# Linear attention and a gated MLP in one kernel: one more unit loaded by squares, six weight sums placed later, and two more decayed keys turned through DRAM

## The chip, the cores and the metric

The kernel runs on one core of a Trainium2 chip. The engines are TensorE (PE in the profile), VectorE (DVE), ScalarE (ACT), GpSimd (POOL) and SyncE (SP); SP, ACT and POOL also issue DMA transfers. The metric is device time in microseconds. Three executions of the kernel before gave 600.44, 600.48 and 600.49 us, median 600.48. A further execution was taken with the hardware profiler.

## The reference

The inputs q, k, v and f_logit have the shape (4 batches, 8 heads, 768 positions, 48 columns). With f = sigmoid(f_logit), every head keeps a 48 by 48 state and gives

```python
for t in range(S):
    state = f[:, :, t, :, None] * state + np.einsum('bhd,bhe->bhde', k[:, :, t], v[:, :, t])
    y[:, :, t] = np.einsum('bhd,bhde->bhe', q[:, :, t], state)
```

The outputs of the 8 heads are laid side by side, which gives x with 3072 tokens and 384 columns, and then

```python
g = x @ w_gate                      # 384 -> 1536
silu = g * (1.0 / (1.0 + np.exp(-g)))
val = x @ w_val                     # 384 -> 1536
return (silu * val @ w_out)         # 1536 -> 384
```

The three weight matrices come as 64-bit floats. The kernel converts them to 32-bit floats on the chip.

## The kernel before, in words

**Units.** The 768 positions are cut into 6 chunks of 128. A unit is one chunk of one batch, so there are 24 units; unit u has chunk u // 4 and batch u % 4 (B = 4). The second chunk holds units 4 to 7, the third units 8 to 11. The 8 heads of a unit are handled as 4 pairs (HP = 4).

**Attention of a unit.** `attention(u)` (L560) is a generator; its parts between two `yield`s are placed one by one. The gates f and their products along the chunk are needed with the head's columns on the partitions and time along the free dimension. The work in order: sigmoid of f (L601 or L608, ScalarE); a scan from the right, "tails" (L630, VectorE) and a reciprocal (L633); kT = k times tails (L576); a scan from the left, "gates" (L658); qT = q times gates (L576); the scores sc = kT by qT (L676, TensorE); the mask A = sc times causal (L691, VectorE, two instructions); y from the carried state (L712) and from A and v (L716, or L737 for the last batch of a chunk); the state's increment dS = kt by v (L757), where kt is the decayed k turned back to time on the partitions; and the new state (L764, L766). "least" (L656 or L683) is a small copy of the chunk's whole decay, from which `decay` makes "decayed". The outputs y reach the layout of the MLP's input xT through DRAM (L720 copies and L727 DMAs, 'xT<-yT'), while the last batch of a chunk goes through a "diagonal" tile (L737).

**Two ways to load.** A plain unit loads f, k and q with time on the partitions (L455) and TensorE transposes them: fTp, kTp and qTp (L596, four instructions each, one for a head pair). A unit "by squares" loads each of f, k and q with four DMAs into squares of 32 rows (L447), and VectorE transposes the squares (L611 for f, L622 for k, L662 for q). `by_squares(u)` is `u >= SQUARES * B - 2`, with SQUARES = 2, so units 6 and up. Loads by squares of units 6 and 7 are issued by POOL, those of later chunks by SP. All v loads but those of units 6 and 7 are issued by SP. A queue's transfers are issued in program order.

**Two ways to turn the decayed k.** Unless `turned` holds, TensorE transposes kT into a bank ("kt", L680, four instructions) and ScalarE copies it out (L689). Where it holds (units 6 and 7, and the fourth and fifth chunk), VectorE transposes kT by squares (L646), four DMAs write it to DRAM ("turn", L649) and one DMA loads it back as kt (L687). `turn_queue` is POOL for the second chunk and SP later.

**The weights.** A piece of the 64-bit weights is loaded by SP into one of four buffers (w64). ScalarE makes two tiles of it, "up" (L489) and "top" (L491), from two buffers each; VectorE joins them by a clamp (L500), a shift (L502), a 16-bit mask (L504) and an add (L506). In the profile these carry the output names w_both (w_gate and w_val together) and w_out. `weights()` issues one piece's fetch, one piece's sizes (ScalarE) and one piece's join (VectorE).

**The MLP.** For the first chunk, `mlp_plain` runs products x by w_gate and x by w_val (L812: 12 of each, three matmuls of 128 by 512 per product, into four banks), silu (L822), the multiplication h = silu times val (L826), and then down products (L835). From the second chunk on, `mlp_fifteen` makes the products of three blocks by three blocks with 15 instead of 18 products (L1014), from sums of the input (xs) and sums of the weights; `down_seven` (L1113, L1176) does the down product with 7 instead of 8. The sums of the weights are VectorE's: `weight_sums(odd)` lists 16 for each half (into "extra" and in place into w_both), and `down_weight_sums` lists four for w_out (ws1, ws2, w_out, ws4).

**What sets the order.** Up to the first three products of the first MLP, an order written out by hand is kept on all engines (`in_order(mark, ...)`). Then `take_turns` runs the steps of `mlp_plain(0)`, with `weights` between them, in turn with the steps of the second chunk's attention; the scheduler may move instructions there, and `keep_order` adds dependencies that hold some of them in order. `behind` holds the instructions of a step behind the VectorE instruction traced last. Three pairs of weight sums are inserted among the h products, the other 13 pairs are woven into the last steps of the down product. From the third chunk on, the order comes from due times: SCORES gives each unit's time and bank kind for its scores ("b", "o" or "A"), CHAINS the times of the steps before, DOWN_SUMS_AT those of the four w_out sums, and `times(c)` the rest; `down[i]` is the i-th half step of the down product. All four lists of steps are merged by time.

Of the kernel before, what the change touches and what calls it, by code (L numbers as in the profile page):

```python
# [9 lines left out]
FP32 = mybir.dt.float32  # L10
# [280 lines left out]
def short_path(ctx, tc, ident, least, judge, q, k, v, f_logit, moe_w_gate, moe_w_val, moe_w_out, out):  # L291
# [9 lines left out]
    nc = tc.nc  # L301
    B, H, S, D = q.shape
    C = 128
    NCH = S // C
    HP = H // 2
# [58 lines left out]
    def pairs(t, off=0):  # L364
        return t[:, off:off + HP * N1].rearrange("p (a t) -> p a t", t=N1)
# [33 lines left out]
    rooms = {nm: t.rearrange("p n h w -> p (n h w)")[:, 0:Q + HP * RUN] for nm, t in both_raw.items()}  # L399

    def by_squares(u):
        return u >= SQUARES * B - 2

    def make_rooms(pool):
        for nm in "fkq":
# [21 lines left out]

    traced = nc.cur_bb.bb.instructions
    by_pool = []

    def load(u, what="fkqv"):
        b, c = units[u]
        rows = slice(c * C, (c + 1) * C)
        inputs = dict(f=f_logit, k=k, q=q, v=v)
        for nm in "fqkv" if c >= SQUARES else "fvkq" if by_squares(u) else "fkqv":
            src = inputs[nm]
            if nm not in what:
                continue
            if nm == "v":
                dst = v_of(u)  # L440
            elif not by_squares(u):
                dst = raw[nm][u % NRAW]
            else:
                since = len(traced)
                for n in range(4):
                    at = Q * (1 - n % 2)
                    (nc.sync if c >= SQUARES else nc.gpsimd).dma_start(  # L447
                        out=rooms[nm][Q * n:Q * (n + 1), at:at + HP * RUN].rearrange("t (a e) -> t a e", a=HP),
                        in_=src[b, n // 2::2, rows, :].rearrange("a (t i) d -> t a (i d)", i=NI))
                if c < SQUARES:  # L450
                    by_pool.extend(ins for ins in traced[since:] if ins.engine == mybir.EngineType.Pool)
                    keep_order(by_pool[-5:])
                continue
            queue = nc.gpsimd if c < SQUARES and by_squares(u) else nc.sync
            queue.dma_start(out=dst[:, :, 0:D], in_=src[b, :, rows, :].rearrange("h t d -> t h d"))  # L455

    def weight_piece(dst, src, parts):

        b, a, n = dst.shape[1:]
        if src.dtype == FP32:
            by_row = src.rearrange("p a (b n) -> p a b n", n=n)
            return (lambda: [nc.sync.dma_start(out=dst[:, :, i], in_=by_row[:, i]) for i in range(a)]), [], []
        shape = [128, b // parts, a, n]
        kept = {}

        def fetch():  # L470
            kept["w"] = wst.tile([128, a, 2 * b * n], I32, tag="w64", name="w64", bufs=4)
            nc.sync.dma_start(out=kept["w"], in_=src)

        def part(m):
            return slice(m * b // parts, (m + 1) * b // parts)

        def halves(m):
            words = kept["w"].rearrange("p a (b n two) -> p a b n two", two=2, n=n)[:, :, part(m)].rearrange("p a b n two -> p b a n two")
            return words[:, :, :, :, 0], words[:, :, :, :, 1]

        def high_ends(m):
            quarters = kept["w"].bitcast(U16).rearrange("p a (b n four) -> p a b n four", four=4, n=n)[:, :, part(m)]
            return quarters.rearrange("p a b n four -> p b a n four")[:, :, :, :, 3]

        def sizes(m):
            lo, hi = halves(m)
            up = wst.tile(shape, I32, tag="up", name="up", bufs=NPART)
            ends = up.bitcast(U16).rearrange("p b a (n two) -> p b a n two", two=2)
            nc.scalar.activation(ends[:, :, :, :, 0], lo.bitcast(U32), AF.Copy, scale=2.0 ** -29)  # L489
            top = wst.tile(shape, I32, tag="top", name="top", bufs=NPART)  # L490
            nc.scalar.activation(top.bitcast(FP32), hi.bitcast(FP32), AF.Abs)  # L491
            kept["up", m], kept["top", m] = up, top

        def join(m, what=("clamp", "add")):
            lo, hi = halves(m)
            up, top = kept["up", m], kept["top", m]
            if "add" in what and "clamp" not in what:
                nc.vector.tensor_tensor(dst[:, part(m)].bitcast(I32), top, up, ALU.add)
                return
            nc.vector.tensor_scalar(top.bitcast(FP32), top.bitcast(FP32), as_float(0x38000000), as_float(0x47F00000),  # L500
                                    op0=ALU.max, op1=ALU.min)
            nc.vector.tensor_scalar(top, top, 3, 0x3FFFFFFF, op0=ALU.logical_shift_left, op1=ALU.bitwise_and)  # L502
            ends = up.bitcast(U16).rearrange("p b a (n two) -> p b a n two", two=2)
            nc.vector.tensor_single_scalar(ends[:, :, :, :, 1], high_ends(m), 0xC000, op=ALU.bitwise_and)  # L504
            if "add" in what:
                nc.vector.tensor_tensor(dst[:, part(m)].bitcast(I32), top, up, ALU.add)  # L506

        return fetch, [lambda m=m: sizes(m) for m in range(parts)], [lambda *what, m=m: join(m, *what) for m in range(parts)]
# [51 lines left out]
    def attention(u):  # L560
# [51 lines left out]
            load_after(u, "f")  # L612
        yield

        turned = SQUARES < c < NCH - 1 or c < SQUARES and in_squares
        turn_queue = nc.sync if c >= SQUARES else nc.gpsimd
        kT = att.tile([128, HP, C], FP32, tag="kT", name="kT")
        qT = att.tile([128, HP, C], FP32, tag="qT", name="qT", bufs=2)
# [9 lines left out]
        for part in parts:  # L628
            at = slice(part.start * N1, part.stop * N1)
            nc.vector.tensor_tensor_scan(tail[:, at][:, ::-1], gate[:, at][:, ::-1], floor[:, at][:, ::-1], 1.0,  # L630
                                         op0=ALU.mult, op1=ALU.max)
        whole = pairs(tail)[:, :, 1:2]
        nc.vector.reciprocal(pairs(start)[:, :, 0:1], whole)  # L633
        yield
# [18 lines left out]

        if in_squares:

            nc.scalar.copy(least[:, u, :], whole.rearrange("p a t -> p (a t)"))  # L656
            whole = least[:, u, :].unsqueeze(2)
        nc.vector.tensor_tensor_scan(gate[:, 0:n], gate[:, 0:n], start, 1.0, op0=ALU.mult, op1=ALU.add)  # L658
        yield
        if in_squares:  # L660
            qp = tail[:, 0:HP * C]
# [1 line left out]
            load_after(u, "qv" if c < SQUARES else "q")  # L663
        yield
        multiply(qT, qp, pairs(gate)[:, :, 1:N1])
        nc.gpsimd.memset(pairs(gate)[:, :, 0:1], 0.0)  # L666
        if c < SQUARES:
            decay()
# [8 lines left out]
        if c < NCH - 1 and not turned:  # L677
            p = bank("kt")
            for a in range(HP):
                nc.tensor.transpose(p[:, a * C:(a + 1) * C], kT[:, a, :], ident)  # L680
        yield
        if not in_squares:
            nc.scalar.copy(least[:, u, :], whole.rearrange("p a t -> p (a t)"))  # L683
        if c < NCH - 1:
            kt = att.tile([128, HP * C], FP32, tag="kt", name="kt")
            if turned:
                turn_queue.dma_start(out=kt, in_=turn.rearrange("t i a r e -> i t (a r e)"))  # L687
            else:
                nc.scalar.copy(kt, p)  # L689
# [73 lines left out]
        if c == 0:  # L763
            nc.scalar.copy(states[b], dS)  # L764
        elif c < NCH - 1:
            nc.vector.tensor_tensor(states[b], decayed[:, :, 0:D], dS, ALU.add)  # L766
        yield

    def load_after(u, what):
# [36 lines left out]
    def mlp_plain(c):  # L806
# [17 lines left out]
        def val(j):  # L824
            p = product(w_val, j, "val")
            nc.vector.tensor_tensor(part(j), part(j), p, ALU.mult)  # L826

        return ([lambda j=j, f=f: f(j) for f, j in ((gate, 0), (val, 0), (gate, 1), (val, 1))] +
                [lambda j=j, f=f: f(j) for i in range(2, NF, 2) for f in (gate, val) for j in (i, i + 1)],
# [49 lines left out]
    def chain(k, q, qmul, turn=None, head=None):  # L879
# [3 lines left out]
    between = [n * TRIPLE - 0.05 for n in range(NJ)]  # L883
    down = [NJ * TRIPLE + n * DOWN / 2 - 0.05 for n in range(14)]
    SCORES = {c: scores for c, scores in zip(range(2, NCH), (
        ((12, "b"), (between[2], "o"), (down[2], "A"), (down[6], "A")),
        ((PRODUCT - 0.05, "b"), (between[1], "o"), (between[3], "o"), (down[3], "A")),
        *[((down[10] - whole, "A"), (between[1], "o"), (between[3], "o"), (down[3], "A"))] * (NCH - 4)))}
    CHAINS = {c: chains for c, chains in zip(range(2, NCH), (
# [18 lines left out]
        return {"o": banks_o, "A": banks_a}[kind].tile([128, 512], FP32, tag=kind, name="sc")  # L908

    FINISH = (3, 5, 6, 7, 9, 10)  # L910
    DOWN_SUMS_AT = (13.1, 26.5, 38, 48)
    sums = {}

    def plus(dst, a, b):
# [278 lines left out]
    def behind(f):  # L1193

        n = len(traced)
        last = next(ins for ins in reversed(traced) if ins.engine == mybir.EngineType.DVE)
        f()
        keep_order([last] + [ins for ins in traced[n:] if ins.engine == mybir.EngineType.DVE])

    def take_turns(first, second, rest):  # L1200

# [77 lines left out]
    joins.pop(0)()  # L1279
    hidden[1]()  # L1280
    weights()
    load(B + 1)
    hidden[2]()
    steps.pop(0)()
    in_order(mark, (mybir.EngineType.PE, mybir.EngineType.DVE, mybir.EngineType.Activation, mybir.EngineType.SP))
# [5 lines left out]
    for i in range(len(joins) - hidden.count(weights)):  # L1291
        last.insert(3 * i, weights)
    sums_of = [weight_sums(odd) for odd in range(2)]
    for n, at in enumerate((5, 6, 8)):
        hidden.insert(hidden.index(weights, 3 * at), lambda n=n: behind(lambda: [t[n]() for t in sums_of]))
    take_turns(hidden + weave(last, sums_of[0][3:7] + sums_of[1][3:7] + sums_of[0][7:] + sums_of[1][7:]), steps, 8)
    assert not fetches and not joins

    early.close()
# [126 lines left out]
```

## Time and profile before

| what | value |
|---|---|
| median of three executions | 600.48 us |
| the profiled execution | 600.68 us |
| its span | 599.0 us |
| TensorE busy | 588.3 us (98%) |
| VectorE busy | 481.7 us (80%) |
| ScalarE busy | 293.6 us (49%) |
| GpSimd busy | 94.3 us (16%) |
| mean granted TensorE clock | 0.999 of full speed |

The span is the time from the first to the last record of the profiled execution; 1.7 us of that execution's time lie around it. Busy time of TensorE is modelled and pipelined, so that a matmul's start to the next one's start tells its price better than its duration. A number in square brackets at the end of a line of the timeline is the idle time of the engine before that instruction, with what released it.

By its own timeline, the first chunk's attention fills TensorE up to 29.07 us, the first MLP's gate and val products run from there to 101.93 us, its down products from 101.93 to 140.22 us, and the 15-product stages follow. The second chunk's attention lies among the first MLP's products: unit 5's f transposes at 55.35, its k and q transposes at 70.93, its scores at 77.47 and its kt transposes at 78.56 us; unit 6's scores at 104.60, unit 7's at 121.06. In the third chunk, unit 10's scores are at 204.38 and unit 11's at 215.94 us.

### The profile page before, as it was taken

What the parts mean: (1) busy time and instruction counts of PE and PEld (TensorE: products, weight loads), DVE (VectorE), ACT (ScalarE), POOL (GpSimd) and SP (SyncE); (2) the same over time, 40 slices, a digit from 0 to 9 for tenths busy, and PEclk for the clock granted to TensorE, in tenths of its full rate; (3) what the DMA queues carried; (4) which work ended last, traced back from release to release, by engine and by line L of the source; (5) the groups of instructions that cost most, each with busy time, mean ns of one, the idle gap of its engine ahead of it and who ended that gap; (6) DMA issues with size and microseconds to landing.
All of it is one profiled execution on the core that took longest, in us unless ns stands there. A gap on an engine that the chain in (4) does not pass through costs nothing.

```text
span 599.0 us, 10862 instructions
## 1 busy us (share of the span) xinstructions
PE 588.3 (98%) x3996; PEld 485.4 (81%) x3996; DVE 481.7 (80%) x834; ACT 293.6 (49%) x558; POOL 94.3 (16%) x211
## 2 busy tenths in 40 slices
PE   7899999999999999999999999999999999999996
PEld 5744545667888899888899888899988899988896
DVE  7999998978999977998995978995878972666731
ACT  3577854115776422576740566632376730356600
POOL 1102225100030230121130030320030320000000
PEclk9999999999999999999999999999999999999999
DMA  9999664124331244442344432343230100100001
GB/s 198 252 274 319 199 182 116 25 77 132 81 83 49 51 110 112 133 97 70 98 116 108 126 76 68 98 112 99 82 102 26 28 10 6 54 1 1 1 1 55
DMA packets 104058, 57.33 MB, mean 96 GB/s; under 512 B 65632, under 2 KB 95712, under 8 KB 104000
## 3 DMA queue, kind: packets, MB, share of 16 engines
q1 hardware_dynamic: 95552, 46.09, 29.3%
q0 software_dynamic: 6432, 7.75, 4.4%
q10 hardware_dynamic: 2016, 2.75, 1.3%
q8 instruction: 32, 0.52, 0.4%
q14 instruction: 26, 0.21, 0.1%
HBM read 46.27 MB, written 7.34 MB: 90 GB/s over the span
## 4 chain that ended last, share of the span: by engine, by line
PE 86%; DVE 0%; issue 0%
PE o L1113 20%; PE A L1014 18%; PE B L1014 14%; PE c L1014 6%; PE o L1014 6%; PE o L835 5%; PE sc L676 3%; PE o L1176 3%; PE y L716 2%; PE gate L812 2%; PE val L812 2%; PE y L737 1%; PE y L712 1%; PE dS L757 1%; PE kt L680 0%; DVE A L691 0%
## 5 line engine op out<-in xcount | busy, mean ns | idle before, releaser
L727 POOL DMA_DIRECT2D xT<-yT x120 | 60.0, 507 | 51.0 <-ACT yT L720 45.2
L1014 PE MATMUL A<-xs,w_both 128*128 128x256 f32 x240 | 62.2, 382 | 0.0
L1113 PE MATMUL o<-w_out,h 128*128 128x192 f32 x360 | 62.0, 327 | 0.0
L1113 PEld LDWEIGHTS o<-w_out,h 128*128 128x128 f32 x360 | 58.7, 190 | 1.2 <-DVE h L966 0.3
L1019 ACT COPY c<-A 128x512 f32<-128x512 f32 x40 | 23.3, 583 | 60.7 <-PE A L1014 60.7
L1019 ACT COPY aside<-A 128x512 f32<-128x512 f32 x60 | 35.2, 586 | 34.1 <-PE A L1014 33.9
L915 DVE TENSOR_TENSOR c<-c,aside 128x512 f32<-128x512 f32 x60 | 41.1, 685 | 12.2 <-ACT aside L1019 10.7
L1014 PEld LDWEIGHTS A<-xs,w_both 128*128 128x128 f32 x240 | 44.9, 190 | 6.6
L966 DVE TENSOR_TENSOR h<-h,c 128x256 f32<-128x256 f32 x100 | 40.5, 414 | 7.6 <-ACT h L1030 7.3
L691 DVE TENSOR_TENSOR A<-sc,causal 128x512 f32<-128x512 f32 x48 | 31.0, 686 | 15.7 <-PE sc L676 15.7
L918 DVE TENSOR_TENSOR c<-c,aside 128x512 f32<-128x512 f32 x60 | 41.0, 683 | 2.2 <-ACT aside L1019 2.1
L1030 ACT ACTIVATE h<-c 128x256 f32<-128x256 f32 x100 | 39.2, 416 | 6.6 <-DVE c L915 5.1
L1113 PE MATMUL o<-ws,h 128*128 128x192 f32 x240 | 41.5, 328 | 0.2 <-DVE A L691 0.2
L666 POOL MEMSET gates<- 128x4 f32 x24 | 3.1, 128 | 243.7 <-DVE qT L576 237.5
L1014 PE MATMUL B<-xs,w_both 128*128 128x256 f32 x160 | 41.2, 380 | 0.0
L1014 PE MATMUL A<-xs,extra 128*128 128x256 f32 x160 | 41.2, 380 | 0.0
L1014 PE MATMUL c<-xT,w_both 128*128 128x256 f32 x160 | 41.1, 379 | 0.0
L1014 PE MATMUL B<-xT,extra 128*128 128x256 f32 x160 | 41.1, 379 | 0.0
L1113 PEld LDWEIGHTS o<-ws,h 128*128 128x128 f32 x240 | 39.1, 190 | 0.8 <-DVE A L691 0.4
L1019 ACT COPY aside<-B 128x512 f32<-128x512 f32 x60 | 35.1, 585 | 8.3 <-PE B L1014 7.1
L918 DVE TENSOR_TENSOR c<-o,c 128x512 f32<-128x512 f32 x40 | 27.4, 685 | 12.6 <-ACT h L1030 6.6
L915 DVE TENSOR_TENSOR c<-c,o 128x384 f32<-128x384 f32 x15 | 8.3, 552 | 36.3 <-PE o L1113 36.3
(154 smaller groups left out, 1224.3 us busy)
## 6 DMA issues: line engine op xcount, KB each, us to landing
fsquares<-in_f_logit_dram SPq DMA_DIRECT2D x64, 96.0 KB, 2.4
qsquares<-in_q_dram SPq DMA_DIRECT2D x64, 96.0 KB, 2.2
ksquares<-in_k_dram SPq DMA_DIRECT2D x64, 96.0 KB, 2.4
w<-in_moe_w_gate_dram SPq DMA_DIRECT2D x6, 768.0 KB, 6.2
w<-in_moe_w_val_dram SPq DMA_DIRECT2D x6, 768.0 KB, 5.3
w<-in_moe_w_out_dram SPq DMA_DIRECT2D x6, 768.0 KB, 6.9
v<-in_v_dram SPq DMA_DIRECT2D x22, 192.0 KB, 3.0
out_dram<-ob ACTq DMA_DIRECT2D x14, 192.0 KB, 2.0
```

What stands on the lines that cost most here:

```text
L676: nc.tensor.matmul(sc[par][:, a * C:(a + 1) * C], lhsT=kT[r, a, :], rhs=qT[r, a, :], start=True, stop=True)
L691: nc.vector.tensor_tensor(A[:, par], sc[par].rearrange("p (a t) -> p a t", t=C), causal.unsqueeze(1).broadcast_to((128, HP, C)), ALU.mult)
L727: (nc.gpsimd if c >= SQUARES else nc.sync).dma_start(out=xT[c][f % 128:f % 128 + n, f // 128, b * C:(b + 1) * C], in_=yT[r:r + n, par, a / ...
L812: nc.tensor.matmul(p, lhsT=w[:, j, i, :], rhs=xT[c][:, i, :], start=(i == 0), stop=(i == KT - 1))
L835: nc.tensor.matmul(p, lhsT=hidden_tile(h, n // 2)[:, n % 2 * 2 + b // 2, b % 2 * C:(b % 2 + 1) * C], rhs=w_out[:, j, :], start=(n == 0), s ...
L915: nc.vector.tensor_tensor(dst, a, b, ALU.add)
L918: nc.vector.tensor_tensor(dst, a, b, ALU.subtract)
L966: lagging.append(lambda: f(*args))
L1014: nc.tensor.matmul(p[name][:, n, :], lhsT=weights_of[a][:, n, j, :], rhs=tokens[b], start=fresh and n == 0, stop=True, skip_group_check=True)
L1019: nc.scalar.copy(t, p[name])
L1030: nc.scalar.activation(dst, src[:, 0, :], AF.Silu)
L1113: nc.tensor.matmul(p[:, n, :], lhsT=lhsTs[j][:, n * C:(n + 1) * C], rhs=rhs[:, j, :], start=first and j == order[0] and n == 0, stop=j == ...
```

## The change

- `by_squares` holds from unit 5 on, so unit 5 (the second chunk's second batch) is loaded by squares. Its three sets of transposes on TensorE and its kt transposes fall away; POOL issues its 12 square loads, and its kT is turned through DRAM on POOL's queue as for units 6 and 7. The "least" copy of units by squares in the second chunk goes from ScalarE to VectorE.
- v of units 1 to 9 is loaded by POOL's queue.
- The first three pairs of weight sums leave the h products and are woven with the others behind the last h. Dependencies put unit 7's right-hand scan behind the last but one h, its left-hand scan behind the last h, and the woven sums from unit 6's new state on behind unit 7's qT. The 16-bit masks of w_out's joins stand behind unit 5's qT.
- `turned` holds for units 10 and 11 too, on SP's queue. For turned units of the third chunk and later, but for the last batch, the kt load is issued with the scores instead of a step later.
- Unit 11's scores have the due time of `down[5]` instead of `down[6]`; the w_out sums have the due times 1.4, 13.1, 26.5 and 48 instead of 13.1, 26.5, 38 and 48.

```diff
     def by_squares(u):
-        return u >= SQUARES * B - 2
+        return u >= SQUARES * B - 3
...
-            queue = nc.gpsimd if c < SQUARES and by_squares(u) else nc.sync
+            queue = nc.gpsimd if nm == "v" and 0 < u < SQUARES * B + 2 else nc.sync
             queue.dma_start(out=dst[:, :, 0:D], in_=src[b, :, rows, :].rearrange("h t d -> t h d"))
...
             nc.vector.tensor_single_scalar(ends[:, :, :, :, 1], high_ends(m), 0xC000, op=ALU.bitwise_and)
+            for ins in first_scores if n == DM else ():
+                keep_order([ins, traced[-1]])
...
-        turned = SQUARES < c < NCH - 1 or c < SQUARES and in_squares
+        turned = SQUARES * B + 2 <= u < (NCH - 1) * B or c < SQUARES and in_squares
...
                                          op0=ALU.mult, op1=ALU.max)
+        if u == SQUARES * B - 1:
+            keep_order([last_of_h[0], traced[-1]])
...
-            nc.scalar.copy(least[:, u, :], whole.rearrange("p a t -> p (a t)"))
+            (nc.scalar.copy if c >= SQUARES else nc.vector.tensor_copy)(least[:, u, :], whole.rearrange("p a t -> p (a t)"))
...
         nc.vector.tensor_tensor_scan(gate[:, 0:n], gate[:, 0:n], start, 1.0, op0=ALU.mult, op1=ALU.add)
+        if u == SQUARES * B - 1:
+            keep_order([last_of_h[1], traced[-1]])
...
         multiply(qT, qp, pairs(gate)[:, :, 1:N1])
+        if u == SQUARES * B - 1:
+            for ins in woven_sums[since[0]:]:
+                keep_order([traced[-1], ins])
+        if u == B + 1:
+            first_scores.append(traced[-1])
...
+        if c < NCH - 1:
+            kt = att.tile([128, HP * C], FP32, tag="kt", name="kt")
+        at_once = turned and c >= SQUARES and b < B - 1
+        if at_once:
+            turn_queue.dma_start(out=kt, in_=turn.rearrange("t i a r e -> i t (a r e)"))
         yield
...
-        if c < NCH - 1:
-            kt = att.tile([128, HP * C], FP32, tag="kt", name="kt")
+        if c < NCH - 1 and not at_once:
...
             nc.vector.tensor_tensor(states[b], decayed[:, :, 0:D], dS, ALU.add)
+            if u == SQUARES * B - 2:
+                since.append(len(woven_sums))
...
             nc.vector.tensor_tensor(part(j), part(j), p, ALU.mult)
+            if j >= NF - 2:
+                last_of_h.append(traced[-1])
...
-        ((12, "b"), (between[2], "o"), (down[2], "A"), (down[6], "A")),
+        ((12, "b"), (between[2], "o"), (down[2], "A"), (down[5], "A")),
...
-    DOWN_SUMS_AT = (13.1, 26.5, 38, 48)
+    DOWN_SUMS_AT = (1.4, 13.1, 26.5, 48)
...
-        keep_order([last] + [ins for ins in traced[n:] if ins.engine == mybir.EngineType.DVE])
+        sums = [ins for ins in traced[n:] if ins.engine == mybir.EngineType.DVE]
+        keep_order([last] + sums)
+        keep_order([last_of_h[-1], sums[0]])
+        woven_sums.append(sums[0])
...
-    load(B + 1)
     hidden[2]()
...
-    for n, at in enumerate((5, 6, 8)):
-        hidden.insert(hidden.index(weights, 3 * at), lambda n=n: behind(lambda: [t[n]() for t in sums_of]))
-    take_turns(hidden + weave(last, sums_of[0][3:7] + sums_of[1][3:7] + sums_of[0][7:] + sums_of[1][7:]), steps, 8)
+    take_turns(hidden + weave(last, sums_of[0][0:7] + sums_of[1][0:7] + sums_of[0][7:] + sums_of[1][7:]), steps, 8)
```

In the resulting instruction order TensorE makes unit 5's scores one gate product later than before and its y and dS two products later; unit 6's scores come after two down steps instead of one, and unit 7's after seven instead of six.

More of the change, by code (lines that the diff above doesn't have):

```diff
@@ L429, in short_path @@
     by_pool = []
+    first_scores = []
+    last_of_h = []
+    woven_sums = []
+    since = []
     def load(u, what="fkqv"):
```

## The prediction

> **What bounds the kernel now.** I read the page's busy shares and its closing chain first, then TensorE's waits, then the timelines at the places the diff touches. The page:
>
> ```profile
> PE 588.3 (98%) x3996; PEld 485.4 (81%) x3996; DVE 481.7 (80%) x834; ACT 293.6 (49%) x558; POOL 94.3 (16%) x211
> ...
> PE 86%; DVE 0%; issue 0%
> ```
>
> TensorE is the bound, and the chain is its instruction stream. The waits of TensorE (us in total, times, longest) show how little it loses:
>
> ```profile
> PE idle L362 <- DVE floor L354: 2.1, 1, 2.1
> PE sc L676 <- DVE qT L576: 1.9, 2, 1.1
> PE sc L676 <- ACT least L683: 0.5, 1, 0.5
> PE sc L676 <- ACT state L764: 0.4, 1, 0.4
> PE sc L676 <- ACT top L491: 0.3, 1, 0.3
> PE y L737 <- issue: 0.3, 1, 0.3
> PE o L1113 <- DVE A L691: 0.2, 1, 0.2
> ```
>
> All but two of these lie before 29.07 us. So time falls only where TensorE instructions or the two later waits go, and rises where a new wait appears. TensorE's timeline (start, duration, instruction):
>
> ```profile
> 55.35 0.60 PE L596 MATMUL fTp<-idf,fraw 128*128 128x128 f32 x4
> ...
> 70.93 0.60 PE L596 MATMUL kTp<-idf,kraw 128*128 128x128 f32 x4
> 71.37 0.60 PE L596 MATMUL qTp<-idf,qraw 128*128 128x128 f32 x4
> ...
> 77.47 1.16 PE L676 MATMUL sc<-qT,kT 48*128 48x128 f32 x16 [0.35 <-ACT top L491]
> 78.56 0.66 PE L680 MATMUL kt<-idf,kT 128*128 128x128 f32 x4
> ...
> 205.47 0.66 PE L680 MATMUL kt<-idf,kT 128*128 128x128 f32 x4
> ...
> 217.03 0.66 PE L680 MATMUL kt<-idf,kT 128*128 128x128 f32 x4
> 217.87 0.92 PE L1113 MATMUL o<-ws,h 128*128 128x192 f32 x4 [0.19 <-DVE A L691]
> ```
>
> These transposes are what the change removes. Matmuls overlap, so the price is start to next start.
>
> **TensorE, removed.** For unit 5 the f transposes cost 55.78−55.35 = 0.43, k and q 71.81−70.93 = 0.88, kt 79.05−78.56 = 0.49. For unit 10 kt costs 205.97−205.47 = 0.50. For unit 11 kt and the wait behind it run from 217.03 to 217.87, 0.84. That wait goes too: sc of unit 11 now comes a down step (2.03) earlier, and half a step on the o bank stands between it and the step that needs the masked A bank. The 0.35 before sc of unit 5 goes, because sc stands one product (2.58) later. Sum 3.49, say 3.5 us.
>
> **VectorE around unit 5.** Added: the f transpose 0.95, and k, q and the turn at 0.62 each, together 2.8; three "least" copies (0.10 to 0.2 each on ACT's rows) 0.3 to 0.6. Moved away: six sums of 0.60, 3.6. Net, it is no fuller before the last h; cost 0. The new pair of order there keeps the u16 parts (0.49) of w_out's joins behind qT of unit 5. In the new order they stand later anyway, and sc of unit 5 has 2.58 more, so 0; 0.4 if qT is still late (the row of the wait that goes).
>
> **The six sums behind the last h.** They add 3.6 us to VectorE where it idled (start, duration, [idle before, releaser]):
>
> ```profile
> 105.79 1.29 DVE L691 TENSOR_TENSOR A<-sc,causal 128x512 f32<-128x512 f32 x2 [2.91 <-PE sc L676]
> ...
> 129.91 0.35 DVE L766 TENSOR_TENSOR state<-decayed,dS 128x192 f32<-128x192 f32 x1 [3.62 <-PE dS L757]
> ```
>
> Idle 2.91+3.62 = 6.53, so 2.9 is left. Without that cover the masks of units 6 and 7 and the xs sums before 140.22 come late, one for one. The tail scan and gate scan of unit 7 now wait for h products; behind them stand its q transpose and qT, read by sc at 121.06, over 10 us after. Cost 0. The down sum moved to 1.4 falls into idle of 0.37 and 0.73 before the ob copies (139.13, 140.42): 0.
>
> **Units 10 and 11.** VectorE does one more transpose (0.62) for each; each unit's four turn DMAs and kt load join SP's queue. SP carries no v loads up to unit 9 any more, and the kt load is issued with the scores. A turn lands 2.3 after issue, a kt load in 5.8 at most: 8.1. From sc to dS of unit 10 is 204.38 to 215.38 less 0.50, 10.5 us; for unit 11 it is 13 or more. Cost 0. But qT of unit 11 ended at 213.06, now 0.62 later, 213.68, and sc arrives at 215.94−0.50−2.03 = 213.41. VectorE gets about 0.6 back from a sum moved out of this stretch. Ends 0 and 0.35 (0.27 and a latency); I take 0.1, near the balance.
>
> **ACT: the step I distrust.** ACT gives up unit 5's gates and kt copy and takes a table load, a sigmoid and another switch early, about 1.28+0.63+1.28 = 3.2, into idle of 1.67+1.51 at 41.85 and 43.56: 0. Later, in the new order, the last but one w_out piece's up and top, a table load, unit 7's sigmoid and a table load all stand ahead of the silu that frees a bank (of four) for a gate product. Rows of ACT's timeline before:
>
> ```profile
> 86.50 1.08 ACT L489 ACTIVATE up<-w 128x768 uint16<-128x768 uint32 x1 [4.61 <-DVE w_both L506]
> ...
> 90.47 0.60 ACT L822 ACTIVATE h<-gate 128x512 f32<-128x512 f32 x1
> 91.08 1.28 ACT L601 ACT_TABLE_LOAD   x1
> 92.38 0.63 ACT L601 ACTIVATE fraw<-fraw 128x512 f32<-128x512 f32 x1
> ```
>
> Start to start: up 0.92, top 0.83, load 1.30, sigmoid 0.53, load 1.30, silu 0.48, 5.36 together. The gate product before was the one at 91.52+2.58 = 94.10. It now stands before y and dS of unit 5 (2.07), and 0.43+0.88+0.49+0.35 = 2.15 is gone ahead of it: 89.88. So up must start by 84.5. It needs the piece landed. SP issues that piece behind the last xT DMA of unit 4, which shares a semaphore with a weight load issued near 70; that lands 6.9 later, the rest of the queue follows, and I place the piece's issue at 78.8 (77.8 to 80). The DMA rows of 54 to 105 us (KB each, median us to landing):
>
> ```profile
> w<-in_moe_w_out_dram SPq DMA_DIRECT2D x6, 768.0 KB, 6.9
> fraw<-in_f_logit_dram POOLq DMA_DIRECT2D x8, 96.0 KB, 5.5
> ```
>
> 78.8+6.9 = 85.7, so TensorE waits 1.2 at that gate. Ends: 0 (landing by 84.5) and 2.8 (issue 80, landing 0.4 above the median). I take 1.2.
>
> **POOL and the start.** POOL's queue takes 12 square loads, one turn and kt load, and v of units 1 to 5, 8 and 9. Unit 5's f is issued near 32; at 5.5 it lands near 38, before ACT's gap. v1 to v3 now run beside f1 to q2. Before, the first 20 us moved 230 GB/s on one queue, so three v (192 KB, 0.85 each) take 2.6 us of the engines; f2 landed at 10.29 and is read at 12.37. With all 2.6 ahead of it, 12.85: 0.5 late. But SP's queue sheds v1, and a wait of 0.48 at 15.08 absorbs a slip. I take 0; ends −0.1 and +0.5.
>
> [...]
>
> **Sum.** −3.5+1.2+0.1 = −2.2. The profiled execution took 600.68 (span 599.0 and 1.7 around), 0.2 above the median of 600.48; it becomes 598.5, the median 598.3.
>
> **Rivals.**
> No new wait (the piece lands by 84.5): −3.5+0.1, 597.1. For it: ACT was idle 4.61 before 86.50, so it isn't short of time. Against: that piece must land 5.2 us before ACT's old reading of it.
> Gain given back: the wait is 2.8 and unit 11's 0.35 and the start's 0.5 come with it: −3.5+3.65 = +0.15, 600.6, within what this measurement can tell from no change (0.2%, 1.2 us).
> Slower: POOL's square loads. The sigmoids of units 6 and 7 stand in ACT's queue ahead of silus that free TensorE's banks. If POOL's loads land 5.5 later than 5.5 after issue, that is past ACT's idle (4.61), and each microsecond more is TensorE's. At 5 us later the gain is spent (−3.5 against the weights' 2.8 and 0.7 here); at 6 to 7, about +1.3 to +2.5, 602 to 603. For it: 16 more transfers on a queue that already takes 5.5. Against: unit 5's have long landed when unit 6's are issued.
>
> **How the numbers follow.** Forecast (0.4 to 2.4 of wait) 0.50; no new wait 0.24; gain given back 0.13; slower 0.13. The forecast's own range is 597.4 to 599.4. The range reaches from 596.7 (no wait, the start 0.1 better, 0.3 for unlisted idle) to 600.7, leaving out the slower case and a little of the low end. Faster by over 0.2% (below 599.28) takes the no-wait case and nearly all of the forecast, 0.73; same 0.14; slower 0.13.
>
> **What would show it.** In the changed kernel's profile: no kt, kTp or qTp group on TensorE for unit 5; no wait of sc on ACT top and none of o on A; near 89 us a gate product waiting for an ACT silu by about 1.2, and ACT's up before it released by a weight DMA. The VectorE idle before state of unit 7 should fall below 1.5 with no TensorE wait between 100 and 140. The first gate product should still start within 0.5 of 29.07. I am wrong if TensorE waits for sc of unit 7, for the first 15-product stage at 140, or for A or kt of units 10 and 11, or if 29.07 slips more.

## The result, and the profile after

The changed kernel took 607.75 us (606.87 to 607.94, four runs) against 600.49 us for the kernel before in the same comparison: a ratio of 1.0116, with a 95% interval of 1.0104 to 1.0128. The prediction was 598.3 us with a range up to 600.7; the kernel became 7.3 us slower instead of 2.2 us faster.

(A correction to the description ahead of the prediction: the transfers 'xT<-yT' go from on-chip memory to on-chip memory; DRAM takes no part in them. Nothing in the prediction's numbers rests on it.)

The page of the changed kernel (busy time per engine, then the rows of TensorE and of its granted clock in 40 slices of 15.2 us):

```profile
PE 590.9 (97%) x3972; PEld 484.5 (80%) x3972; DVE 485.6 (80%) x843; ACT 291.5 (48%) x552; POOL 111.2 (18%) x235
...
PE   7899987999999999999999999999999999999996
...
PEclk9999996999999999999999999999999999999999
```

TensorE executes 24 instructions less and is 2.6 us longer busy. TensorE's row dips in the sixth and seventh slice, 76 to 106 us, and the clock's in the seventh. TensorE's waits (us in total, times, longest) name it:

```profile
PE gate L833 <- DVE h L847: 3.5, 1, 3.5
PE gate L833 <- ACT h L843: 2.3, 1, 2.3
PE idle L362 <- DVE floor L354: 2.1, 1, 2.1
PE sc L691 <- DVE qT L582: 1.1, 2, 0.8
PE fTp L602 <- DMA fraw<-in_f_logit_dram: 0.8, 2, 0.5
```

The two upper lines are new. So is the last one, which lies in the first 20 us and belongs to the start. The two waits that were to go, 0.3 before unit 5's scores and 0.2 before o at 217.87, are gone as forecast. TensorE's timeline there (start, duration, instruction, [idle before, releaser]):

```profile
82.36 5.31 PE L833 MATMUL val<-xT,w_both 128*128 128x512 f32 x12
89.95 4.54 PE L833 MATMUL gate<-xT,w_both 128*128 128x512 f32 x6 [2.27 <-ACT h L843]
97.94 5.49 PE L833 MATMUL gate<-xT,w_both 128*128 128x512 f32 x6 [3.45 <-DVE h L847]
103.36 0.79 PE L731 MATMUL y<-qT,decayed 48*64 48x128 f32 x16
```

The two gate products behind the waits last 4.54 and 5.49 us; two such products together took 5.42 before, at 91.52. The windows of TensorE (stretch, busy time, granted clock, DMA share, GB/s) tell why:

```profile
89.00:90.00 1.00, 0.05 (x1) 1.00 0.21 80
90.00:91.00 1.00, 1.00 (x2) 0.51 0.05 18
...
94.00:95.00 1.00, 0.49 (x2) 1.00 0.00 0
...
96.00:97.00 1.00, 0.00 (x0) 0.92 0.32 66
97.00:98.00 1.00, 0.06 (x1) 0.50 0.34 74
102.00:103.00 1.00, 1.00 (x2) 0.50 0.77 184
104.00:105.00 1.00, 1.00 (x24) 1.00 0.08 25
```

The clock is granted at 0.50 with the end of the first wait and from inside the second on, and stays there for 3.4 and 6.8 us. So a wait is paid twice here: once as idle time, once in the matmuls behind it.

Held against the trace of before at the same instructions, the account is this. The first gate product is 0.28 late. Unit 5's removed work and wait give 0.43+0.88+0.49+0.35 = 2.15. The waits take 2.27+3.45 = 5.72. The slow matmuls take 4.54−2.74 = 1.80, then (103.36−97.94)−2.58 = 2.84, then 0.12 in y: 4.76. That makes +8.6; the first 15-product stage starts at 149.09 instead of 140.22, +8.88 (the 0.3 left over I put down to the ends of matmuls, from which the two waits are counted: the two gate products at 79.05 of before last 5.32 by their ends and 5.16 from start to start). Units 10 and 11 give 1.36 back by 237 us, which leaves +7.52, and the rest of the span gives back 0.4: the spans differ by 606.1−599.0 = 7.1.

What held the two gate products? ScalarE's and VectorE's timelines of the changed kernel:

```profile
79.81 0.93 ACT L495 ACTIVATE top<-w 128x768 f32<-128x768 f32 x1
87.62 1.06 ACT L493 ACTIVATE up<-w 128x768 uint16<-128x768 uint32 x1 [6.89 <-DMA w<-in_moe_w_out_dram]
88.55 0.86 ACT L495 ACTIVATE top<-w 128x768 f32<-128x768 f32 x1
89.31 0.59 ACT L843 ACTIVATE h<-gate 128x512 f32<-128x512 f32 x1
```

```profile
84.73 0.14 DVE L664 COPY least<-tails 128x4 f32<-128x4 f32 x1
89.44 0.56 DVE L504 TENSOR_SCALAR top<-top 128x768 f32<-128x768 f32 x1 [4.58 <-ACT top L495]
...
97.21 0.67 DVE L847 TENSOR_TENSOR h<-h,val 128x512 f32<-128x512 f32 x1
```

ScalarE's in-order queue waits 6.89 us for the fourth w_out piece, and the silu behind it (89.31), whose gate product had ended at 78.67, is what the first late gate product needs. VectorE waits in turn 4.58 us for that piece's top; behind it stand unit 6's chain and more joins, and only then the ninth h product (97.21), which frees the bank of the last gate product; its silu had ended at 89.90 and its val product by 87.67. SyncE's queue shows when the piece was issued (start, time until the last of the group is issued):

```profile
56.00 14.64 SPq L476 DMA_DIRECT2D w<-in_moe_w_out_dram  x3
70.84 6.88 SPq L746 DMA_DIRECT2D xT<-yT  x10
77.82 1.89 SPq L476 DMA_DIRECT2D w<-in_moe_w_out_dram  x3
```

Three w_out pieces go out ahead of unit 4's ten xT transfers and three behind them; in the kernel before it was four and two:

```profile
55.56 11.66 SPq L472 DMA_DIRECT2D w<-in_moe_w_out_dram  x4
68.46 8.15 SPq L727 DMA_DIRECT2D xT<-yT  x10
76.73 1.04 SPq L472 DMA_DIRECT2D w<-in_moe_w_out_dram  x2
```

### The profile page after: what moved, and what is told of

It is laid out like the page before. It is cut to its first block, busy times and chain, and to the rows that moved or that the text cites. A ratio compares the mean times of both kernels' runs of the same rounds, so it can differ in the third digit from the quotient of the medians.

```text
span 606.1 us, 10863 instructions
## 1 busy us (share of the span) xinstructions
PE 590.9 (97%) x3972; PEld 484.5 (80%) x3972; DVE 485.6 (80%) x843; ACT 291.5 (48%) x552; POOL 111.2 (18%) x235
## 4 chain that ended last, share of the span: by engine, by line
PE 85%; DVE 9%; DMA 3%; issue 1%; ACT 1%; POOL 0%; DVEq 0%; ACTq 0%; POOLq 0%
PE o L1136 20%; PE A L1037 18%; PE B L1037 14%; PE c L1037 6%; PE o L1037 6%; PE o L858 5%; PE sc L691 4%; PE o L1199 3%; PE y L735 2%; DMA w<-in_moe_w_out_dram 2%; PE y L756 2%; PE y L731 1%; PE dS L776 1%; DVE top L506 1%; DVE w_both L512 1%
## 5 line engine op out<-in xcount | busy, mean ns | idle before, releaser
L833 PE MATMUL gate<-xT,w_both 128*128 128x512 f32 x72 | 37.2, 665 | 5.7 <-DVE h L847 3.5
```

The lines of the kernel that those rows point to most:

```text
L833: nc.tensor.matmul(p, lhsT=w[:, j, i, :], rhs=xT[c][:, i, :], start=(i == 0), stop=(i == KT - 1))
```

## The experiments

Theories: A, the late issue of the fourth piece on SyncE's queue is the cause; B, POOL's additional loads slow that piece down; C, VectorE's own in-order queue holds the ninth h, whatever the piece does. The medians, each beside runs of the kernel before on the same chip (600.49 us for the change, 600.6 to 600.75 for the others):

| kernel | median us | ratio to before (95%) | last gate product's wait | ninth h on VectorE |
|---|---|---|---|---|
| before | 600.5 | | none | 93.19 |
| the change | 607.75 | 1.0104 to 1.0128 | 3.45 | 97.21 |
| second chunk's part alone | 608.91 | 1.0123 to 1.0157 | 5.13 | 96.59 |
| third chunk's part alone | 599.60 | 0.9977 to 0.9996 | none | 93.12 |
| two pieces issued early | 604.17 | 1.0040 to 1.0073 | 3.12 | 93.06 |
| waits filled with matmuls | 604.76 | 1.0045 to 1.0078 | 0.46 | 97.50 |
| ninth h early | 599.74 | 0.9969 to 1.0004 | none | 89.69 |
| both edits | 597.37 | 0.9921 to 0.9961 | none | 86.09 |
| both edits, v1 to v3 on SyncE | 598.25 | 0.9944 to 0.9970 | none | 86.33 |
| the change, v1 to v3 on SyncE | 607.58 | 1.0075 to 1.0140 | 5.33 | 97.14 |
| six sums alone | 600.11 | 0.9980 to 0.9999 | none | 89.97 |
| the change without the six sums | 599.27 | 0.9969 to 0.9989 | 0.81 | 93.07 |

**The two parts of the change.** Third chunk's part alone, by its edit of the kernel before:

```diff
-        turned = SQUARES < c < NCH - 1 or c < SQUARES and in_squares
+        turned = SQUARES * B + 2 <= u < (NCH - 1) * B or c < SQUARES and in_squares
...
+        at_once = turned and c >= SQUARES and b < B - 1
...
-        ((12, "b"), (between[2], "o"), (down[2], "A"), (down[6], "A")),
+        ((12, "b"), (between[2], "o"), (down[2], "A"), (down[5], "A")),
...
-    DOWN_SUMS_AT = (13.1, 26.5, 38, 48)
+    DOWN_SUMS_AT = (1.4, 13.1, 26.5, 48)
```

> The kernel before with the third chunk's part of the change alone: kT of units 10 and 11 turned through DRAM, the kt load with the scores, unit 11's scores at the earlier due time, the new due times of the w_out sums. Both theories: no new wait, 0.50 and 0.84 us of TensorE less, 599.1 (598.9 to 599.4). Rival: sc of unit 11 waits for its qT, or dS of units 10 or 11 for kt, and 0.4 to 1 us of it is lost, 599.5 to 600.1.

Measured: 599.60 us. That is outside the expected range and inside the rival's; but the kernel before took 600.75 on this chip, so the gain is 1.15, 0.2 less than the 1.34 expected. In the trace this kernel is 1.42 ahead by 283 us, 1.36 of it from the two places, and the rival's waits are not there. TensorE's timeline of this kernel:

```profile
213.41 1.16 PE L676 MATMUL sc<-qT,kT 48*128 48x128 f32 x16
214.50 2.22 PE L1117 MATMUL o<-w_out,h 128*128 128x192 f32 x12
216.55 4.06 PE L1117 MATMUL o<-ws,h 128*128 128x192 f32 x24
```

There is no bracket behind any of them: the scores of unit 11 come at 213.41, the time that the prediction had worked out, and wait for nothing; the kt transposes and the wait on A are gone. In the trace this part did what it was to do.

The second chunk's part alone is the changed kernel with those four edits undone.

> The changed kernel without the third chunk's part (unit 5 by squares, v loads on POOL, six sums behind the last h, nothing else). If the two parts add up, as the traces say (8.88 us lost by 149 us, 1.36 gained at units 10 and 11): 609.1 (608.3 to 609.9), with both waits near 88 and 94 us. If the third chunk's part had a hand in the loss: nearer to 600.

Measured: 608.91 us. The parts add up within the noise, and the loss belongs to the second chunk's part. (The waits of this kernel were 1.56 on the silu and 5.13 on the h.)

**The late piece.** In the changed kernel, two fetches are put ahead of the xT transfers; the order on the other engines is the same, instruction by instruction:

```diff
             nc.sync.dma_start(out=kept["w"], in_=src)
+            fetched.append(traced[-1])
+            if 16 <= len(fetched) <= 17:
+                for ins in first_out:
+                    keep_order([traced[-1], ins])
...
+                    if u == B:
+                        first_out.append(traced[-1])
                     f += n
```

> The changed kernel, with one thing moved: on SP's queue the fourth and fifth w_out piece are issued ahead of unit 4's ten xT transfers instead of behind them (the order on all other engines is the same). Theory A, the late issue on SP's queue: in the changed kernel the fourth piece is issued at 77.82 us and ACT waits 6.89 us for it until 87.62. Here its issue is held only by its buffer, about 73.8, the fifth near 77.8; they land by 80 and 84, TensorE's two waits (2.27 and 3.45) and the half-speed stretches behind them go but for at most 1.2 us, and the time is 597.0 to 598.6. Theory B, POOL's loads of the same time take the DMA engines: the pieces land at 86 or later whatever their issue, and the time is 606 to 608.

Measured: 604.17 us, 3.6 below the changed kernel but 5.6 above what theory A alone expected. (The traced execution, at 602.70, was the fastest of four; the others took 604.16 to 604.39.) SyncE's queue, then TensorE and VectorE:

```profile
56.41 18.11 SPq L478 DMA_DIRECT2D w<-in_moe_w_out_dram  x5
74.57 11.42 SPq L752 DMA_DIRECT2D xT<-yT  x10
```

```profile
87.92 2.74 PE L841 MATMUL gate<-xT,w_both 128*128 128x512 f32 x6
93.79 4.54 PE L841 MATMUL gate<-xT,w_both 128*128 128x512 f32 x6 [3.12 <-DVE h L855]
```

```profile
92.58 0.58 DVE L514 TENSOR_SCALAR up<-w 128x768 uint16<-128x768 uint16 x1
93.06 0.67 DVE L855 TENSOR_TENSOR h<-h,val 128x512 f32<-128x512 f32 x1
```

The wait on the silu is gone: the piece's issue made that one, and it is shown. Theory B falls as a cause of its own: with POOL's loads unchanged, up of the fourth piece now starts at 82.63 instead of 87.62 and waits for no weight. Whether those loads have a share in the 9.7 us that the late piece took to land isn't shown, since no run leaves them out. But the wait on the ninth h stays, 3.12 us, with the clock at 0.50 behind it. VectorE's timeline lists no idle time between 60 and 95 us now; no transfer holds it. Its ninth h starts at 93.06, and in the kernel before it started at 93.19, so VectorE is no later than before. What has changed is when TensorE needs it. Two rows of before:

```profile
93.19 0.67 DVE L826 TENSOR_TENSOR h<-h,val 128x512 f32<-128x512 f32 x1
```

```profile
96.78 5.31 PE L812 MATMUL val<-xT,w_both 128*128 128x512 f32 x12
```

By the semaphores in the trace of before, the last gate product (94.10) waits for ScalarE alone: its bank is one that a silu frees, the one of 90.47. The val product at 96.78 waits for VectorE, so it takes the bank that the ninth h frees at 93.86, 2.92 us ahead of it. In the changed kernel the last gate product waits for VectorE's semaphore, and the val product behind it for ScalarE's: the two have changed banks. So TensorE wants the bank of the ninth h 6.8 us earlier: 2.58 for one product, 2.15 for the removed work, and 2.07 because y and dS of unit 5 have moved behind it. The margin was 2.92. With the start 0.69 late in this execution and the h 0.13 earlier, that makes a wait of 3.06; 3.12 was measured.

**VectorE's order.** In the changed kernel, the ninth h is put ahead of unit 6's kT and left-hand scan, unit 7's f transpose and the joins of the last three pieces:

```diff
+    def behind_h(mine):
+        after_h.extend(mine)
+        for ins in mine if ninth else ():
+            keep_order([ninth[0], ins])
...
+            if kept["n"] >= 16:
+                behind_h([ins for ins in traced[n:] if ins.engine == mybir.EngineType.DVE])
...
+            if j == NF - 4:
+                ninth.append(traced[-1])
+                for ins in after_h:
+                    keep_order([traced[-1], ins])
```

> The changed kernel with VectorE's order altered: the ninth h product (its bank is the one that the last gate product waits for) stands ahead of unit 6's kT and left-hand scan, of the joins of the last three w_out pieces and of unit 7's f transpose. Theory C, VectorE is packed and its in-order queue holds that h behind other work: the wait of 3.45 us and the slow product of 5.42 behind it go, the wait of 2.27 on ACT (the late w_out piece) stays: about 6 us back, 601.7 (601 to 602.5). Theory A alone (only the late piece matters): the h moves no further than the piece lets it, 606 to 608.

Measured: 599.74 us, 8.0 below the changed kernel and 2 below what was expected. TensorE:

```profile
83.03 5.31 PE L852 MATMUL val<-xT,w_both 128*128 128x512 f32 x12
89.71 5.42 PE L852 MATMUL gate<-xT,w_both 128*128 128x512 f32 x12 [1.36 <-ACT h L862]
95.06 0.67 PE L750 MATMUL y<-qT,decayed 48*64 48x128 f32 x16
```

Of the two waits here one is left, on the silu behind the still late piece (up starts at 87.37), and it is 1.36 us long, because TensorE comes some 0.7 later (an earlier gate product waits 0.61 for its silu now). The clock stays at 1.00 behind both, which is where most of the 2 us that I had not expected come from. Theory C is shown for the wait that is gone; theory A holds for the wait that is left.

**Both edits together.**

> Both edits: the fourth and fifth w_out piece issued ahead of unit 4's xT transfers, and the ninth h early on VectorE. If the late piece and VectorE's order are the whole loss of the second chunk, no TensorE wait over 0.5 is left between 30 and 150 us, the clock stays at 1.00 and the time is the prediction's sum without new waits plus the start's slip of 0.3 to 0.7: 597.3 to 598.3. If a third cause is hidden behind them (the masks of unit 7, the sums behind the last h), TensorE waits between 100 and 150 us and the time is over 599.

Measured: 597.37 us, a ratio of 0.9941 (0.9921 to 0.9961): faster than both kernels. Its waits of TensorE, all of them before 30 us, and the two gate products:

```profile
PE idle L362 <- DVE floor L354: 2.1, 1, 2.1
PE sc L716 <- DVE qT L601: 1.9, 2, 1.1
PE sc L716 <- ACT least L728: 0.5, 1, 0.5
PE y L783 <- issue: 0.4, 1, 0.4
PE sc L716 <- ACT state L810: 0.4, 1, 0.4
```

```profile
87.55 5.31 PE L860 MATMUL gate<-xT,w_both 128*128 128x512 f32 x12
```

Nothing is hidden behind the two causes: no wait between 100 and 150 us, though the six sums now fill VectorE behind the last h. At the first 15-product stage this kernel is 1.81 ahead of the kernel before, at 280 us 3.17.

**The clock.** In the changed kernel, TensorE gets matmuls of no use in its two waits:

```diff
+            n = len(traced)
+            if j >= NF - 2:
+                idle = aps.tile([128, 512], FP32, tag="a", name="idle")
+                for _ in range((9, 20)[j - NF + 2]):
+                    nc.tensor.matmul(idle, lhsT=floor.bitcast(mybir.dt.bfloat16)[:, 0:128],
+                                     rhs=floor.bitcast(mybir.dt.bfloat16)[:, 0:512], start=True, stop=True)
...
+            if j >= NF - 2:
+                mine = [ins for ins in traced[n:] if ins.engine == mybir.EngineType.PE]
+                keep_order(products[-1:] + mine)
+            products.append(traced[-1])
```

> The changed kernel with 9 and 20 small matmuls of no use (128x512, bf16, into a free bank) ahead of the two gate products at which TensorE waits, so that it is not idle there. Theory A: the granted clock of 0.50 after each wait follows from the idle time itself. Then the clock stays at 1.00 and the gate product of 5.42 us takes 2.6; the slow product ahead of it lies before a wait and gives nothing; about 2.8 us come back, 604.9 (604.4 to 605.3). Rival: the low clock has another cause (the load of the other engines, the place in the program), then the clock still falls and the time is 607.7 or a little more.

Measured: 604.76 us, 3.0 below the changed kernel. The timeline of TensorE, where 9 and 20 matmuls now lie in the waits:

```profile
88.77 2.11 PE L847 MATMUL idle<-floor 128*128 128x512 bf16 x9
90.71 2.74 PE L834 MATMUL gate<-xT,w_both 128*128 128x512 f32 x6
93.29 4.48 PE L847 MATMUL idle<-floor 128*128 128x512 bf16 x20
98.22 2.84 PE L834 MATMUL gate<-xT,w_both 128*128 128x512 f32 x6 [0.46 <-DVE h L859]
```

The gate products last 2.74 and 2.84 again and the mean clock is 1.000. The low clock is a consequence of the idle time. The wait for the ninth h is no shorter: the matmuls of no use stand in it. The gain is what the second slow product had cost: the first one had lain in front of a wait.

The granted clock in windows of 0.2 us (of 1 us where none of 0.2 was read) gives the edges of each slow stretch. In the changed kernel it is 0.50 from 90.01 to 93.42 and from 96.84 to 103.66: 3.41 and 6.82 long, and 6.83 from start to start, so these four edges lie on one grid of 3.41. With the two early fetches it is 94.41 to 97.82 (3.41), with the second chunk alone 94.51 to 101.33, with v on SyncE 94.84 to 101.67 (6.8 each). In the 3.41 us ahead of each of these five falls TensorE was idle for 2.27, 2.35, 2.80, 2.33 and 2.32 us. The waits of 1.36 (with the ninth h early), 1.56 (second chunk alone) and 2.18 (v on SyncE) brought no fall; why 2.18 brought none and 2.27 did isn't shown. The two stretches of 3.41 had no idle time in them; the three of 6.8 had 1.10, 2.80 and 3.02, all at their start.

**The start and POOL's v loads.**

```diff
-            queue = nc.gpsimd if nm == "v" and 0 < u < SQUARES * B + 2 else nc.sync
+            queue = nc.gpsimd if nm == "v" and B <= u < SQUARES * B + 2 else nc.sync
```

> The changed kernel with v of units 1 to 3 on SP's queue again, nothing else. The late piece and VectorE's order are untouched, so the two waits near 88 and 94 us stay: 607.0 to 607.8. Theory B (POOL's queue is what makes it late) would have it well below 606.

Measured: 607.58 us, as theory A and C have it. The loads that POOL issues near the late piece, those of units 6 and 7, are not touched by this run, so it says nothing against them.

> As the kernel with both edits, and v of units 1 to 3 on SP's queue again as before the change. If those three loads, on POOL's queue at the start, are what delays the first chunk (0.28 us by 29 us in the changed kernel, 0.69 in another run), the first gate product starts at 29.07 again and the time is 0.3 to 0.7 lower than that kernel's, 597.0 to 597.5. If they are not: the same time as that kernel.

Measured: 598.25 us, 0.9 above the kernel without this edit; the intervals of the two overlap. Neither expectation had that, and the traces don't show it: at the first 15-product stage they stand at 138.33 with the edit and 138.41 without. The first chunk's dS of unit 3 stands at 28.52 with the edit and at 28.51 without it, so v on POOL's queue wasn't what delayed the start in that pair. The delay differs between executions with v on POOL (0.08 to 0.79 us). In each one above 0.11, TensorE's waits list an fTp waiting for an f load; but two with 0.08 and 0.11 list one too. Which of the transfers makes the difference wasn't settled; it's worth 0.7 us at most.

**The six sums.** The kernel before with the sums' placing alone:

```diff
-    for n, at in enumerate((5, 6, 8)):
-        hidden.insert(hidden.index(weights, 3 * at), lambda n=n: behind(lambda: [t[n]() for t in sums_of]))
-    take_turns(hidden + weave(last, sums_of[0][3:7] + sums_of[1][3:7] + sums_of[0][7:] + sums_of[1][7:]), steps, 8)
+    take_turns(hidden + weave(last, sums_of[0][0:7] + sums_of[1][0:7] + sums_of[0][7:] + sums_of[1][7:]), steps, 8)
```

> The kernel before with the six sums behind the last h, and nothing else of the change. VectorE has 2.4 us (four sums of 0.60) less ahead of the ninth h, and TensorE's order becomes that of the changed kernel: unit 5's y and dS stand behind the last two gate products, which therefore come 2.07 earlier. Theory C: the ninth h comes as much earlier as its product is wanted, no wait: the same as before, 600.2 to 600.9. Rival, the six sums behind the last h are themselves what is late (masks of units 6 and 7, the first 15-product stage): waits between 105 and 150 us and 601.5 or more.

Measured: 600.11 us, ratio 0.9980 to 0.9999. The ninth h comes at 89.97, 3.2 earlier than before, and the two gate products, which TensorE's order has moved ahead of unit 5's y and dS here too, wait for nothing. The last of them takes a bank of ScalarE's here, as in the kernel before. Moving the sums is harmless by itself.

The changed kernel with the three pairs among the h products again (the diff above, the other way round):

> The changed kernel with the three pairs of sums among the h products again, as before the change. That puts 2.4 us back on VectorE ahead of the ninth h and puts unit 5's y and dS ahead of the last two gate products again (2.07 of cover); the w_out pieces still stand behind unit 4's xT transfers. Theory C: VectorE is fuller than before by 3.5 us of unit 5's chain and TensorE comes 2.15 earlier, so the last gate product waits for the ninth h or the masks of unit 5 for over 3 us: 604 to 610. Rival, the move of the sums made the loss: 598 to 600.

Measured: 599.27 us. My expectation was wrong, and its rival was right: without the move of the sums the loss is gone. Its waits near there:

```profile
PE gate L833 <- ACT h L843: 0.8, 1, 0.8
...
PE o L858 <- DVE h L847: 0.5, 1, 0.5
```

Its last gate product, and VectorE's ninth h:

```profile
93.17 2.84 PE L833 MATMUL gate<-xT,w_both 128*128 128x512 f32 x6 [0.81 <-ACT h L843]
```

```profile
93.07 0.66 DVE L847 TENSOR_TENSOR h<-h,val 128x512 f32<-128x512 f32 x1
```

I had added up VectorE's work ahead of the ninth h, as in the prediction. But in this kernel the scheduler puts other things there: y and dS of unit 5 stand ahead of the last two gate products again (89.51 instead of 87.5 for the first of them), the silu that the changed kernel had behind the fourth piece stands ahead of it (82.81), and the h comes at 93.07. That h is as late as with the two early fetches (93.06), yet it holds nothing: the last gate product starts at 93.17, before the h has ended, and waits for a silu. Its bank is ScalarE's again, as in the kernel before. So neither part of the second chunk's change makes the loss alone. With unit 5 by squares and the sums away, the steps are traced in another rhythm, and the kernel then has four things at once: the last two gate products ahead of y and dS of unit 5 on TensorE, the last of them in the bank that the ninth h frees, the fourth piece behind the xT transfers on SyncE, and silu and h behind that piece on ScalarE and VectorE. No run changes the bank alone, so its share isn't measured by itself. Even so, TensorE's gain of 2.15 at unit 5 is spent here: a start 0.11 late and the two waits, which cost 1.08 and 0.81 from start to start, leave 0.13 of it at the first 15-product stage. Why the orders and the banks come out so wasn't looked into.

## Why the prediction was wrong

- **TensorE, removed** (3.5 us): right. With the waits out of the way, 1.81 is left of 2.15 at the first 15-product stage with a start 0.11 late, and 1.36 of 1.34 at units 10 and 11, in the changed kernel and with the third chunk's part alone. The forecast's sum without new waits, 597.1, is what both edits together reached (597.37).
- **VectorE around unit 5** ("Net, it is no fuller before the last h; cost 0"): this is the step that failed. That VectorE is no fuller came out right (ninth h at 93.06 with the piece early, 93.19 before), although only four of the six sums, 2.4 us, had stood ahead of that h. That the cost is 0 doesn't follow from it. A sum of durations says nothing about when TensorE needs one instruction of an in-order queue. The last gate product, which the prediction itself placed at 89.88, takes the bank that the ninth h frees, and that h had ended at 93.86; the wait of about 4 us was in no term. With the piece early it measured 3.12, in the changed kernel 3.45. The prediction had this product wait for a silu, as it does in the kernel before; in the changed kernel the bank is another.
- **ACT: the step I distrust** (1.2 us, ends 0 and 2.8): the mechanism was seen, and the place and the price were not. A w_out piece issued behind unit 4's xT transfers does arrive late and does hold ScalarE. But it was the fourth piece, not the fifth, and it held the last but one gate product, not the last; its issue at 77.82 was within a microsecond of what I had worked out for the fifth (78.46 measured, 78.8 said); it was up 9.8 after issue, not 6.9, with three pieces issued together where there had been two. And I followed the piece down ScalarE's queue only. VectorE waited for it as well, 4.58 us, with the bank's h behind. The wait of 1.2 turned out 2.27.
- **The clock** was in no term of the sum. At 4.8 us in the trace it cost nearly as much as the waits; the run with filled waits showed 3.0 of it as what TensorE could have had back with the waits left in place.
- **The six sums behind the last h**, cost 0: right as such, no wait between 100 and 150 us in any kernel that had them. What they did to the order ahead of the last h was not seen.
- **Units 10 and 11**, no new wait: right. The 0.1 taken for qT of unit 11 wasn't needed.
- **POOL and the start**: 0.28 in the changed kernel, inside the ends of −0.1 and 0.5; the 0.69 and 0.79 of two other executions were outside. (The 230 GB/s behind the 2.6 us was 217 in the windows of before from 3 to 20 us, which makes 2.7.) The f load of unit 2, which the sum was about, made no wait; those of units 1 and 3 did, 0.36 and 0.48 in the changed kernel.
- **Rivals.** The slower one named POOL's square loads, with a threshold of 5 us of lateness. They weren't late for ScalarE: unit 7's landed by 85.85, and its sigmoid stood at 92.92 because of the weights. With the two pieces issued early they did land late, the last at 89.75, and ScalarE waited 2.66 us for it, but no wait of TensorE came of it. "Gain given back" had the right place and a third of the price.

## What to carry to other kernels

Where TensorE is 98% busy and lists no wait, another engine can still be right behind it: before crediting removed matmuls, find, in the new order, for each bank that TensorE reuses next the instruction that frees it, and how long before its use that ends. The bank of a product can change with the order, as it did here. Credit only what that margin leaves, or move that instruction forward with the same edit; here two edits of order turned a loss of 1.2% into a gain of 0.6%. Every wait of 2.27 us or more in the stage had a stretch of 3.4 or 6.8 us at half speed with it, half of whose busy part is lost (1.8 and 3.0 in the changed kernel); so price such a wait with that stretch.

## What the runs showed of the hardware

The granted clock was 0.50 in five stretches, each with a wait of TensorE just ahead of it or at its start: two of 3.41 us and three of 6.8. In the changed kernel their four edges lie on one grid of 3.41. In the 3.41 us ahead of each fall TensorE had been idle for 2.27 to 2.80 us; waits of 1.36, 1.56 and 2.18 brought no fall. The stretches of 3.41 had no idle time in them, those of 6.8 had 1.10 to 3.02. So two waits of nearly one length can differ: 2.18 had no slow stretch behind it, 2.27 had one that cost 1.8. What made the difference isn't shown; no run varied one wait alone. A product of three 128x512 matmuls, 2.58 us at full clock, took up to 5.42 in the slow stretch. Idle time that was filled with matmuls of no use kept the clock at 1.00 in the one kernel that had them.
